# Interleaved head columns with their gate logits, rows of 640, one division per pair, and an earlier second table in an attention and expert kernel

## The chip, the cores and the metric

The kernel runs on one core of one Trainium2 chip, as one program. The metric is the device time of an execution in microseconds (us), and the time of a kernel is the median of its runs. Engines are named as the profile names them: PE (matmuls), PEld (its weight loads), DVE, ACT, POOL, and SP, which here only issues DMAs.

## The reference, cut to what matters

Attention over 8 batches, 8 heads, 576 positions and 64 columns per head comes first, and a mixture of experts with one expert per token stands on its output. In short:

```python
q_rot, k_rot = rotate(q), rotate(k)
attn = softmax(q_rot @ k_rot.T / sqrt(64))           # per batch and head
x = (attn @ v).transpose(0, 2, 1, 3).reshape(4608, 512)
logits = x @ w_gate                                   # 8 experts
e_idx = argmax(logits); gate_w = softmax(logits)[e_idx]
eom = sigmoid(x @ w_output_gate)
out[t] = gate_w[t] * eom[t, e] * (relu(x[t] @ w1[e]) @ w2[e]),  e = e_idx[t]
```

## The kernel before, in words

**Attention.** The work goes by pairs of heads, 32 of them, four to a batch. A pair has nine score tiles. For each, PE makes the scores (line 571), DVE takes the row maximum (576), ACT the exponential with its row sum (590), and DVE transposes the result by 32x32 blocks (598). PE then multiplies with the values into `acc`, one PSUM tile with a single buffer (621). At the end of a pair ACT copies `acc` to SBUF (629 to 631), and `back` writes into the same PSUM banks again: per chunk of 128 queries one PE transpose, which brings the queries to the partitions (640), and one small matmul with the gate weights, which gives that pair's share of the router's logits (642). `divide` then divides by the softmax's sums into `xb`, the batch's block in SBUF: one DVE operation for the 5x128 head columns (652) and one for the 5x32 logit shares (653). The next pair's first value matmul writes `acc` again, so it comes after `divide`. `EVENTS` is a list written out by hand that says in which of the nine steps of a pair, and at which of five places in the step, each of these parts is issued.

**Placing tokens.** When a batch is done, `place` sums the logit shares over the heads (`s0`, line 682), picks the expert (`s1` to `s8`), computes the token's gate (`s9` to `s13`), counts ranks within an expert (`s14` to `s17`) and turns token numbers into a table of lists by one-hot products (`ones` on ACT, `s20` on PE, `s21`). `store` writes `xb` to `xd` in DRAM, a row per token with its gate in the last column: 513 columns, of a block whose rows in SBUF have 640. The small arithmetic is on POOL. For the last batch these functions are not in `PLACES` but in a list, `att.last`, that the expert stage takes pieces from. Three stores of the batch before it (`late`) stand in that list too.

**Experts.** The work is in 26 slots, each of 256 or 128 tokens of one expert. A slot has eight steps j (`slot`, line 1217 on): `first` in j = 0 to 3 (`products`, line 1130 or, for 128 tokens, 1122), `second` in j = 4 to 7 (1173). At j = 4 and 5 `turn` transposes the next slot's tokens (1108). In every step ACT and DVE split a 512 KB block of weights into two parts (1092, 1094; some of the differences are on POOL), and SP loads a later one. `gather` fetches the tokens of slot s + 2 from `xd` by an indirect DMA of POOL, at j = 6; `store` scatters a finished slot's rows, also by POOL, at j = 1 and 4 of the next slot. Slots 0 to 4 hold tokens of the first six batches, by a first table of lists (`table0`) made during the attention. Slots from 5 on need the second table, `table1`: counts and slot bounds (`floor`, `sums`, `taken`, `slots`), the transposed lists written to DRAM (`turned`, 940 to 947), rows of them fetched back by indirect DMA (`rows_of`, 911 and 912) for the slots of 256 (number 2) and of 128 (number 1), and `numbers`, which subtracts and masks on POOL (921 to 924), waits some pieces, and then transposes on PE (931) and converts on DVE (932) to the row numbers that `gather` reads.

**What sets the order.** Each engine runs its instructions in program order. `table1` is a generator, cut at its `yield`s into 70 pieces; `run` takes two pieces from the list `left` at the end of every step j (three in slots 1 and 2). So slot 0 takes pieces 0 to 15, slot 1 takes 16 to 39, slot 2 takes 40 to 63, slot 3 takes 64 to 79. Before, `left` is `att.last` (46 entries with the late stores) and behind it all of `table1`: counts and the slots of number 2 are pieces 46 to 50, the transposed lists 51 and 52, `rows_of(2)` 54, the slots of number 1 at 55 to 57, `rows_of(1)` 58, `numbers(2)` 66 with its transpose at 72, `numbers(1)` 76 and 82. In a step, `turn`, `split`, `load`, `store`, `scaled` and `gather` come ahead of the pieces.

```python
left = att.last + pieces(moe.table1(), 70)
            if j == 6:
                self.gather(s + 2)
            for _ in range(per):
                if left:
                    left.pop(0)()
```

Of the kernel before, what the change touches and what calls it, by code (L numbers as in the profile page):

```python
# [23 lines left out]
P = 128  # L24
# [3 lines left out]
NCH = 5  # L28
XW = DM + 1

HL = 2 * E
RW = DM + H * HL

# [120 lines left out]
def body(ctx, tc, nb, offs, qk, v, rope, cst, gates, w, out):  # L154
# [45 lines left out]
    nc.sync.dma_start(out=stage[:, 0:nst], in_=cst[:, o:])  # L200
    nc.sync.dma_start(out=ii.rearrange("p n (h x) -> p n h x", h=2), in_=gates)

# [67 lines left out]
    if n0:  # L270
        left = att.last + pieces(moe.table1(), 70)
    else:
        left = []
        for f in att.last + pieces(moe.table1(), 70):
            f()
        moe.fetch()
        moe.gather(1)
        moe.begin0()
        moe.begin1()
# [8 lines left out]
class Attention:  # L288


    def __init__(self, tc, nb, pools, cc, ident, ii, first, trib, oneb, cnt, zero, qk, v, xd, row, lists):
# [29 lines left out]
        def newxb(b):  # L321
            xbs[b] = px2.tile([P, NCH, RW], F32, tag="xb", name=f"xb{b}")
        for n, pr in enumerate(self.pairs):
# [98 lines left out]
class Pair:  # L422
# [210 lines left out]
    def back(self):  # L633

        self.bk = self.acc.rearrange("p a b -> p (a b)")
        T, x = self.nc.tensor, [self.ac[:, c, :, :].rearrange("p a x -> p (a x)") for c in range(4)]
        x.append(self.al.rearrange("p a x -> p (a x)"))
        for cs in (range(4), (4,)):
            for c in cs:
                T.transpose(out=self.bk[0:x[c].shape[-1], c * BS:c * BS + P], in_=x[c], identity=self.ident)  # L640
            for c in cs:
                T.matmul(self.bk[0:x[c].shape[-1], c * BS + P:c * BS + P + BW], x[c], self.ii[:, self.hp, :],  # L642
                         start=True, stop=True, skip_group_check=True)

    def divide(self, xb):

        V = self.nc.vector
        heads = lambda a, x: a.rearrange("p c (h x) -> p c h x", x=x)
        r = self.rz.rearrange("p (c h) -> p c h", h=2).unsqueeze(3)
        x0, l0 = self.hp * P, DM + self.hp * 2 * HL  # L650
        five = self.bk[:, 0:NCH * BS].rearrange("p (c x) -> p c x", c=NCH)
        V.tensor_tensor(out=heads(xb[:, :, x0:x0 + P], D), in0=heads(five[:, :, 0:P], D), in1=r.broadcast_to((P, NCH, 2, D)), op=ALU.mult)
        V.tensor_tensor(out=heads(xb[:, :, l0:l0 + 2 * HL], HL), in0=heads(five[:, :, P:P + BW], HL),
                        in1=r.broadcast_to((P, NCH, 2, HL)), op=ALU.mult)

# [7 lines left out]
def place(tc, pools, pairs, b, NT, cc, trib, oneb, cnt, xbs, xd, row, lists):  # L663
# [17 lines left out]
    def s0():  # L681
        nc.vector.tensor_reduce(new("lgs", [P, NCH, 16]), xbs[b][:, :, DM:].rearrange("p c (h x) -> p c x h", x=HL), axis=AX.X, op=ALU.add)

# [53 lines left out]
    def s13(i=None):  # L737

        c = slice(0, NCH) if i is None else slice(2 * i, min(2 * i + 2, NCH))
        V.tensor_copy(xbs[b][:, c, DM], T["eg"][:, c])  # L740

# [85 lines left out]
class Moe:  # L827
# [3 lines left out]
    def __init__(self, tc, nb, pools, cc, ident, cnt, w, xd, lists, lst, out):  # L831
# [5 lines left out]
        self.rows = list_rows(nb) // P  # L837
        self.idx, self.ei, self.ri, self.tk = {}, {}, {}, {}
        self.wr, self.wp, self.xt, self.ht, self.gss, self.pys, self.hrs, self.regs, self.phs, self.ys = ({} for _ in range(10))
# [139 lines left out]
    def table1(self):  # L979
# [29 lines left out]
        yield  # L1009
        if self.n2:  # L1010
            self.rows_of(2, 2 * self.n2)
        yield
        tn, r = t([P, E], "tn"), self.padded("rn")
# [6 lines left out]
        G.tensor_tensor(out=g1, in0=g1, in1=eb, op=ALU.add)  # L1020
        yield
        d1 = self.starts("d1", g1, BIG)
        self.slots(1, e1, d1, g1[:, 0:1], 1)
        self.used = t([1, 1], "used", I32)
        G.tensor_copy(self.used, e1[0:1, E - 1:E])
        yield
        self.rows_of(1, self.n1)
        for _ in range(8):
            yield
        if self.n2:  # L1030
            yield from self.numbers(2, 2 * self.n2, 6)
# [27 lines left out]
    def gather(self, s):  # L1059
        if s >= self.end:  # L1060
            return
        n = self.NT - (2 * S if s < self.n0 else 0)
        for h in range(self.todo[s][0]):
# [33 lines left out]
    def turn(self, s, h):  # L1097
# [3 lines left out]
        if h == 0:  # L1101
            self.xt[s] = [self.buf(f"xt{i}", 0, 1, 1, [P, 4, SLOT], F32R, f"xt{i}_{s}{self.nm}") for i in range(2)]
            self.gss[s] = self.buf("gs", s, 2, 2, [P, 2], F32, f"gs{s}{self.nm}")
            V.tensor_copy(self.gss[s], self.xgs[s % 2][:, :, DM])
        xth, xtl = self.xt[s]
        tp = self.small.tile(f"mtp{s}_{h}{self.nm}")
        for dc in range(4):
            nc.tensor.transpose(out=tp[:, dc, :], in_=self.xgs[s % 2][:, h, dc * P:dc * P + P], identity=self.ident)  # L1108
        hs = slice(h * P, h * P + P)
# [107 lines left out]
    def slot(self, s, left, per=2):  # L1217
        for j in range(8):
# [15 lines left out]
            if j == 7:  # L1234
                self.scaled(s)
                if s == self.end - 1:
                    self.store(s, 0)
                    self.store(s, 1)
            if j == 6:
                self.gather(s + 2)  # L1240
            for _ in range(per):
                if left:
# [24 lines left out]
def layouts(q, k, v, wgt, wog, w1, w2):  # L1267
# [11 lines left out]
    g = np.concatenate([wgt, wog], 1).reshape(NP, 2, D, 2 * E)  # L1279
    gd = np.zeros((P, NP, 2, 2 * E), g.dtype)  # L1280
    for h in range(2):
        gd[h * D:h * D + D, :, h] = g[:, h].transpose(1, 0, 2)
    g = gd
    a = w1.reshape(E, 4, P, 4, 256).transpose(3, 0, 2, 1, 4).reshape(4, E * P, 1024)
    c = w2.reshape(E, 4, 2, P, DM).transpose(1, 0, 3, 2, 4).reshape(4, E * P, 1024)
# [23 lines left out]
```

## Time and profile before

| | |
|---|---|
| median of 3 runs | 1020.32 us (1018.58 to 1023.95) |
| the profiled execution's own time | 1015.65 us |
| its span, first to last instruction | 1013.8 us |
| mean granted TensorE clock | 0.993 |
| busy, share of the span | PE 97%, PEld 86%, DVE 76%, ACT 66%, POOL 59% |
| DMA | 216.55 MB, mean 214 GB/s |

The span is one execution on the chip. Busy time does not count the issuing of DMAs by SP or ACT, nor waits. The attention fills the span to about 514 us, the expert slots the rest. The releaser that the profile puts beside an idle time is inferred from semaphores: where an instruction waits for several, the one that came last by the profile is named, and that can be the engine's own preceding instruction.

### The profile page before, as it was taken

What the parts mean: (1) busy time and instruction counts of PE and PEld (TensorE: products, weight loads), DVE (VectorE), ACT (ScalarE), POOL (GpSimd) and SP (SyncE); (2) the same over time, 40 slices, a digit from 0 to 9 for tenths busy, and PEclk for the clock granted to TensorE, in tenths of its full rate; (3) what the DMA queues carried; (4) which work ended last, traced back from release to release, by engine and by line L of the source; (5) the groups of instructions that cost most, each with busy time, mean ns of one, the idle gap of its engine ahead of it and who ended that gap; (6) DMA issues with size and microseconds to landing.
All of it is one profiled execution on the core that took longest, in us unless ns stands there. A gap on an engine that the chain in (4) does not pass through costs nothing.

```text
span 1013.8 us, 34974 instructions
## 1 busy us (share of the span) xinstructions
PE 984.0 (97%) x14701; PEld 867.2 (86%) x14701; DVE 775.0 (76%) x1010; ACT 673.8 (66%) x1438; POOL 602.3 (59%) x708
## 2 busy tenths in 40 slices
PE   7999999999999999999999989999999999999997
PEld 6888888888888888888798878899898989899886
DVE  6889979989898988988767654657765866857673
ACT  5666686776868768686657643457666765856763
POOL 4886887878888777886615784115333543442532
PEclk9999999999999999999999998999999999999999
DMA  6554474564655455563567965657887978887780
GB/s 218 174 166 159 132 230 132 175 215 131 208 180 160 178 167 189 166 206 109 161 241 275 305 223 187 218 178 274 308 305 223 349 246 279 294 315 276 248 312 30
DMA packets 61961, 216.55 MB, mean 214 GB/s; under 512 B 7844, under 2 KB 10276, under 8 KB 61800
## 3 DMA queue, kind: packets, MB, share of 16 engines
q1 hardware_dynamic: 53360, 192.08, 57.2%
q0 software_dynamic: 7264, 21.31, 5.9%
q8 instruction: 117, 1.92, 0.8%
q10 hardware_dynamic: 1176, 0.89, 0.3%
q14 instruction: 44, 0.36, 0.1%
HBM read 196.10 MB, written 20.24 MB: 213 GB/s over the span
## 4 chain that ended last, share of the span: by engine, by line
PE 81%; ACT 7%; issue 4%; DVE 4%; POOL 2%; DMA 1%; POOLq 0%; ACTq 0%; DVEq 0%
PE sc L571 20%; PE py L1173 18%; PE acc L621 16%; PE ph L1130 14%; PE ph L1122 6%; ACT pm L590 3%; PE acc L642 3%; PE acc L640 2%; DVE m L576 2%; PE mtp L1108 1%; DVE wl L1094 1%; PE htp L1158 1%; ACT wh L1092 1%; ACT pl L795 1%; ACT ro L792 1%
## 5 line engine op out<-in xcount | busy, mean ns | idle before, releaser
L590 ACT ACTIVATE pm<-sc,m 128x576 f32<-128x576 f32 x288 | 210.8, 736 | 132.2 <-DVE m L576 129.9
L1094 DVE TENSOR_TENSOR wl<-wr,wh 128x1024 fp32r<-128x1024 f32 x183 | 229.4, 1276 | 43.6 <-ACT wh L1092 37.8
L576 DVE TENSOR_REDUCE m<-sc 128x1 f32<-128x576 f32 x288 | 207.3, 751 | 51.5 <-PE sc L571 48.0
L1173 PE MATMUL py<-wh,ht 128*128 128x512 f32 x640 | 217.3, 404 | 0.0
L1092 ACT CAST wh<-wr 128x1024 fp32r<-128x1024 f32 x208 | 211.8, 1049 | 0.0
L571 PE MATMUL sc<-kh,q 64*128 64x288 f32 x1024 | 204.2, 316 | 4.6 <-ACT pm L590 3.3
L621 PE MATMUL acc<-pt,v 32*64 32x160 f32 (+1 forms) x9216 | 198.5, 294 | 6.9 <-PE sc L571 5.6
L621 PEld LDWEIGHTS acc<-pt,v 32*64 32x64 f32 x9216 | 160.2, 131 | 30.3 <-issue 18.5
L598 DVE STREAM_TRANSPOSE pt<-pm 128x1152 f32<-128x1152 f32 x128 | 174.5, 1363 | 0.0
L571 PEld LDWEIGHTS sc<-kh,q 64*128 64x128 f32 x1024 | 147.7, 184 | 29.2 <-ACT pm L590 16.0
L1130 PE MATMUL ph<-xt,wh 128*128 128x256 f32 x896 | 161.9, 283 | 0.6 <-DVE xt L1111 0.6
L1173 PEld LDWEIGHTS py<-wh,ht 128*128 128x128 f32 x640 | 120.9, 189 | 26.6 <-DVE ht L1160 0.8
L1130 PEld LDWEIGHTS ph<-xt,wh 128*128 128x128 f32 x896 | 138.5, 189 | 3.2 <-DVE xt L1111 2.0
L1094 POOL TENSOR_TENSOR wl<-wr,wh 128x1024 fp32r<-128x1024 f32 x25 | 63.6, 2546 | 122.7 <-ACT wh L1092 115.2
L571 PE MATMUL sc<-kl,q 64*128 64x288 f32 x512 | 130.8, 292 | 0.0
L1173 PE MATMUL py<-wl,ht 128*128 128x512 f32 x320 | 126.7, 396 | 0.0
L1130 PE MATMUL ph<-xt,wl 128*128 128x256 f32 x448 | 126.1, 282 | 0.0
L1147 ACT ACTIVATE ht<-ph 128x512 fp32r<-128x512 f32 x56 | 33.4, 597 | 85.1 <-PE ph L1130 85.1
L571 PEld LDWEIGHTS sc<-kl,q 64*128 64x128 f32 x512 | 85.5, 185 | 0.0
L1130 PEld LDWEIGHTS ph<-xt,wl 128*128 128x128 f32 x448 | 84.6, 189 | 0.0
L513 POOL TENSOR_TENSOR rk<-rk,rt 128x1152 f32<-128x1152 f32 x31 | 82.1, 2649 | 0.0
L513 POOL TENSOR_TENSOR rq<-rq,rt 128x1152 f32<-128x1152 f32 x31 | 82.1, 2647 | 0.0
(255 smaller groups left out, 1517.8 us busy)
## 6 DMA issues: line engine op xcount, KB each, us to landing
wr<-in_w SPq DMA_DIRECT2D x208, 512.0 KB
v<-in_v SPq DMA_DIRECT2D x64, 576.0 KB
rk<-in_qk SPq DMA_DIRECT2D x31, 576.0 KB
rq<-in_qk SPq DMA_DIRECT2D x31, 576.0 KB
xd<-xb SPq DMA_DIRECT2D x12, 513.0 KB
xd<-xb POOLq DMA_DIRECT2D x4, 513.0 KB
xd<-xb SPq DMA_DIRECT2D x6, 128.2 KB
rk<-in_qk SPq DMA_DIRECT2D x2, 288.0 KB
```

Source lines behind the costliest of these rows:

```text
L513: self.eng(eng).tensor_tensor(out=rv, in0=rv, in1=self.rt[:, 2 * t:2 * t + 2, x], op=ALU.mult)
L571: nc.tensor.matmul(self.ps[i][:, a, :HS], st, mv, start=(n == 0), stop=(n == 2))
L576: nc.vector.tensor_reduce(self.m[i], ps[:, :, :HS], axis=AX.XY, op=ALU.max, negate=True)
L590: nc.scalar.activation(pe.rearrange("p (a b) -> p a b", a=2), self.ps[i][:, :, :HS], AF.Exp, bias=self.m[i], scale=1.0, accum_out=self.z[: ...
L598: self.nc.vector.transpose(out=self.pt[:, st[0]:st[0] + 6:5, :], in_=pe)
L621: nc.tensor.matmul(self.acc[h * D:h * D + D, a, o:o + 32 * n], self.v[r, h, j, :], self.pt[r, u:u + n, 32 * j:32 * j + 32], start=(j == 0) ...
L1092: self.nc.scalar.copy(wh, r)
L1094: eng.tensor_tensor(out=wl, in0=r, in1=wh.bitcast(F32), op=ALU.subtract)
L1122: nc.tensor.matmul(ph[:, 0, :], st[:, dc, 0:P], mv[:, dc, :], start=(n == 0), stop=(n == 11))
L1130: nc.tensor.matmul(ph[:, f, :], st[:, dc, fs], mv[:, dc, :], start=(n == 0), stop=(n == 11))
L1147: nc.scalar.activation(fl(hth[:, js, :]), fl(ph), AF.Relu)
L1173: self.nc.tensor.matmul(py[h], st[:, f, hs], mv, start=(f == 0 and n == 0), stop=(f == 7 and n == 2))
```

## The change

- **Columns.** `back`'s transposes write column x of head h to place 2x + h, so that the two heads take turns: each of the 5 transposes per pair writes PSUM with a step of two words. The gate weights are laid out the same way on the host, so the 32 logit shares stand as (x, h) right behind the 128 columns: 160 columns per chunk, contiguous in PSUM and in `xb`. The rows of w1 are put in the same order on the host.
- **Division.** `divide` is one DVE operation over 5 x 80 x 2 elements. The sums are read as pairs (h), repeated 80 times.
- **Rows.** `xb` and `xd` rows are both 640 columns: four groups of 128 head columns and 32 logit shares. The gate goes to column 128. Stores and gathers move 640 columns, and `turn` takes its four chunks of 128 at a pitch of 160. `s0` sums over two axes, of which the inner one is the pair (h).
- **Second table.** The first five pieces of `table1` run together with entries 25 to 29 of `att.last` (slot 1, j = 3 and 4). Pieces 5 to 8 stand at 46 to 49, ahead of the last batch's three stores, which move from 43 to 45 to 50 to 52. In the generator `rows_of(2)` comes after the sums of number 1 (piece 54 as before), `rows_of(1)` moves behind `numbers(2)` (to 73), `numbers(2)` begins at 64 with its transpose at 73, `numbers(1)` at 78 and 83.
- **Gathers.** `gather(s + 2)` is called at j = 0 and at j = 6, and issues once, at the first call for which the table's numbers exist. For slot 5 that is still j = 6 of slot 3; for all others it is j = 0.

```diff
-XW = DM + 1
+HW = D + 2 * E
+XW = H * HW
-RW = DM + H * HL
+WAIT = 8
...
-        left = att.last + pieces(moe.table1(), 70)
+        f, t = att.last, pieces(moe.table1(), 70)
+        for k in range(5):
+            f[25 + k] = lambda a=f[25 + k], b=t[k]: (a(), b())
+        left = f[:-4] + 4 * [f[17]] + t[5:9] + f[-3:] + t[9:]
...
-                T.transpose(out=self.bk[0:x[c].shape[-1], c * BS:c * BS + P], in_=x[c], identity=self.ident)
+                T.transpose(out=self.bk[0:x[c].shape[-1], c * BS:c * BS + P].rearrange("p (x h) -> p h x", h=2), in_=x[c], identity=self.ident)
...
-        heads = lambda a, x: a.rearrange("p c (h x) -> p c h x", x=x)
-        r = self.rz.rearrange("p (c h) -> p c h", h=2).unsqueeze(3)
-        x0, l0 = self.hp * P, DM + self.hp * 2 * HL
+        x0 = 2 * self.hp * HW
+        heads = lambda a: a.rearrange("p c (x h) -> p c x h", h=2)
+        r = self.rz.rearrange("p (c h) -> p c h", h=2).unsqueeze(2)
         five = self.bk[:, 0:NCH * BS].rearrange("p (c x) -> p c x", c=NCH)
-        V.tensor_tensor(out=heads(xb[:, :, x0:x0 + P], D), in0=heads(five[:, :, 0:P], D), in1=r.broadcast_to((P, NCH, 2, D)), op=ALU.mult)
-        V.tensor_tensor(out=heads(xb[:, :, l0:l0 + 2 * HL], HL), in0=heads(five[:, :, P:P + BW], HL),
-                        in1=r.broadcast_to((P, NCH, 2, HL)), op=ALU.mult)
+        self.nc.vector.tensor_tensor(out=heads(xb[:, :, x0:x0 + 2 * HW]), in0=heads(five[:, :, 0:2 * HW]),
+                                     in1=r.broadcast_to((P, NCH, HW, 2)), op=ALU.mult)
...
-        nc.vector.tensor_reduce(new("lgs", [P, NCH, 16]), xbs[b][:, :, DM:].rearrange("p c (h x) -> p c x h", x=HL), axis=AX.X, op=ALU.add)
+        nc.vector.tensor_reduce(new("lgs", [P, NCH, 16]), xbs[b].rearrange("p c (q x) -> p c q x", q=NP)[:, :, :, P:].rearrange("p c q (x h) -> p c x q h", h=2), axis=AX.XY, op=ALU.add)
...
-        if self.n2:
-            self.rows_of(2, 2 * self.n2)
-        yield
         tn, r = t([P, E], "tn"), self.padded("rn")
...
+        if self.n2:
+            self.rows_of(2, 2 * self.n2)
+        yield
         d1 = self.starts("d1", g1, BIG)
...
-        self.rows_of(1, self.n1)
-        for _ in range(8):
+        for _ in range(WAIT):
             yield
         if self.n2:
-            yield from self.numbers(2, 2 * self.n2, 6)
-        for _ in range(4):
+            yield from self.numbers(2, 2 * self.n2, 9)
+        self.rows_of(1, self.n1)
+        for _ in range(5):
             yield
-        yield from self.numbers(1, self.n1, 6)
+        yield from self.numbers(1, self.n1, 5)
...
-        if s >= self.end:
+        if s >= self.end or s in self.got or self.todo[s][1] not in self.idx:
             return
+        self.got.add(s)
...
-            if j == 6:
+            if j in (0, 6):
                 self.gather(s + 2)
```

## Rows read from the trace of the kernel before

**Rows 1.** Busy time in stretches: start:end, length, PE, PEld, DVE, ACT, POOL, clock, DMA, GB/s

```profile
46.00:107.00 61.00, 60.14 (x1497) 52.23 (x1497) 55.20 (x73) 40.17 (x110) 44.28 (x35) 1.00 0.49 158
565.16:588.95 23.79, 23.79 (x157) 21.57 (x156) 16.05 (x18) 12.36 (x18) 19.74 (x50) 1.00 0.95 308
588.95:620.74 31.79, 26.23 (x156) 23.01 (x155) 14.68 (x17) 11.95 (x16) 22.68 (x50) 0.89 0.56 178
620.74:644.50 23.76, 23.76 (x155) 21.38 (x155) 14.69 (x17) 11.79 (x16) 5.03 (x4) 1.00 0.66 222
```

**Rows 2.** Timeline of PE in slot 3, with idle time and releaser in brackets

```profile
603.49 0.66 PE L1108 MATMUL mtp<-ident,xg 128*128 128x128 f32 x4 [0.23 <-DMA xg<-xd,0idx]
609.48 0.29 PE L931 MATMUL 2tr<-ident,2tk 18*128 18x18 f32 x1 [5.34 <-POOL 2tk L921]
```

**Rows 3.** Busy time in stretches, columns as in rows 1, cut by POOL's work

```profile
553.77:569.22 15.45, 15.45 (x89) 13.19 (x88) 8.51 (x10) 12.43 (x25) 10.11 (x15) 1.00 0.92 252
569.22:583.73 14.51, 14.51 (x101) 13.33 (x100) 9.76 (x12) 7.40 (x12) 12.29 (x42) 1.00 1.01 327
583.73:601.37 17.64, 17.64 (x125) 16.43 (x124) 10.86 (x12) 9.34 (x13) 13.94 (x37) 1.00 0.67 207
601.37:605.64 4.27, 2.54 (x13) 1.65 (x11) 1.75 (x2) 2.20 (x3) 3.32 (x6) 1.00 0.84 271
605.64:609.42 3.78, 0.00 (x0) 0.00 (x0) 1.89 (x3) 0.07 (x1) 3.52 (x5) 0.70 0.54 183
```

**Rows 4.** What wrote tile xg: count, duration ns min/median/max, first and last start

```profile
L1064 POOL DMA_INDIRECT xg<-xd,0idx x10: 1008/1120/1813, 499.8 to 600.1; - x10
```

**Rows 5.** Timeline of POOL in slot 0

```profile
525.07 2.67 POOL L1094 TENSOR_TENSOR wl<-wr,wh 128x1024 fp32r<-128x1024 f32 x1 [4.36 <-ACT wh L1092]
530.30 1.17 POOL L688 TENSOR_TENSOR dd<-lgs,mx 128x40 f32<-128x40 f32 x1 [2.57 <-DVE mx L685]
...
538.94 1.81 POOL L1064 DMA_INDIRECT xg<-xd,0idx  x1 [0.52 <-issue]
541.05 1.45 POOL L1064 DMA_INDIRECT xg<-xd,0idx  x1 [0.30 <-issue]
```

**Rows 6.** The chain that ended last, in slot 0: start, length, what

```profile
530.30 1.18 POOL dd L688
...
531.51 0.24 ACT ex L691
...
536.60 0.50 ACT pl L795
...
537.15 0.39 PE pl L802
```

**Rows 7.** Timeline of DVE at the end of a pair

```profile
182.29 0.78 DVE L652 TENSOR_TENSOR xb<-acc,rz 128x640 f32<-128x640 f32 x1
183.00 0.31 DVE L653 TENSOR_TENSOR xb<-acc,rz 128x160 f32<-128x160 f32 x1
```

**Rows 8.** What wrote and read tile xb, columns as in rows 4

```profile
L653 DVE TENSOR_TENSOR xb<-acc,rz x32: 305/307/316, 45.5 to 519.3; 128x160 f32<-128x160 f32 x32
...
L682 DVE TENSOR_REDUCE lgs<-xb x8: 1214/1223/1253, 97.9 to 528.7; 128x80 f32<-128x640 f32 x8
```

**Rows 9.** Timeline of PE behind the division of rows 7

```profile
183.59 0.67 PE L621 MATMUL acc<-pt,v 32*64 32x160 f32 x27 [0.32 <-PE sc L571]
```

**Rows 10.** Waits of PE from 30 to 514 us: total us, times, longest

```profile
PE acc L621 <- PE sc L571: 5.6, 17, 0.4
```

**Rows 11.** Instructions of line 640, columns as in rows 4

```profile
L640 PE MATMUL acc<-ident,ac x128: 272/273/330, 42.4 to 517.0; 128*128 128x128 f32 x128
L640 PE MATMUL acc<-ident,al x32: 277/277/277, 43.7 to 518.0; 128*64 128x128 f32 x32
```

**Rows 12.** The chain that ended last, through one pair's back

```profile
180.60 0.81 PE acc L642 x8
181.41 0.11 PE acc L640
```

More of the change, by code (lines that the diff above doesn't have):

```diff
@@ L200, in body @@
     nc.sync.dma_start(out=stage[:, 0:nst], in_=cst[:, o:])
-    nc.sync.dma_start(out=ii.rearrange("p n (h x) -> p n h x", h=2), in_=gates)
+    nc.sync.dma_start(out=ii.rearrange("p n (x h) -> p n x h", h=2), in_=gates)
     consts = [
@@ L321, in newxb @@
         def newxb(b):
-            xbs[b] = px2.tile([P, NCH, RW], F32, tag="xb", name=f"xb{b}")
+            xbs[b] = px2.tile([P, NCH, XW], F32, tag="xb", name=f"xb{b}")
         for n, pr in enumerate(self.pairs):
@@ L645, in divide @@
     def divide(self, xb):
-        V = self.nc.vector
-        heads = lambda a, x: a.rearrange("p c (h x) -> p c h x", x=x)
-        r = self.rz.rearrange("p (c h) -> p c h", h=2).unsqueeze(3)
-        x0, l0 = self.hp * P, DM + self.hp * 2 * HL
+        x0 = 2 * self.hp * HW
+        heads = lambda a: a.rearrange("p c (x h) -> p c x h", h=2)
+        r = self.rz.rearrange("p (c h) -> p c h", h=2).unsqueeze(2)
         five = self.bk[:, 0:NCH * BS].rearrange("p (c x) -> p c x", c=NCH)
-        V.tensor_tensor(out=heads(xb[:, :, x0:x0 + P], D), in0=heads(five[:, :, 0:P], D), in1=r.broadcast_to((P, NCH, 2, D)), op=ALU.mult)
-        V.tensor_tensor(out=heads(xb[:, :, l0:l0 + 2 * HL], HL), in0=heads(five[:, :, P:P + BW], HL),
-                        in1=r.broadcast_to((P, NCH, 2, HL)), op=ALU.mult)
+        self.nc.vector.tensor_tensor(out=heads(xb[:, :, x0:x0 + 2 * HW]), in0=heads(five[:, :, 0:2 * HW]),
+                                     in1=r.broadcast_to((P, NCH, HW, 2)), op=ALU.mult)
 def number(NT, b):
@@ L739, in s13 @@
         c = slice(0, NCH) if i is None else slice(2 * i, min(2 * i + 2, NCH))
-        V.tensor_copy(xbs[b][:, c, DM], T["eg"][:, c])
+        V.tensor_copy(xbs[b][:, c, P], T["eg"][:, c])
     def store(i):
@@ L837, in __init__ @@
         self.rows = list_rows(nb) // P
-        self.idx, self.ei, self.ri, self.tk = {}, {}, {}, {}
+        self.idx, self.ei, self.ri, self.tk, self.got = {}, {}, {}, {}, set()
         self.wr, self.wp, self.xt, self.ht, self.gss, self.pys, self.hrs, self.regs, self.phs, self.ys = ({} for _ in range(10))
@@ L1103, in turn @@
             self.gss[s] = self.buf("gs", s, 2, 2, [P, 2], F32, f"gs{s}{self.nm}")
-            V.tensor_copy(self.gss[s], self.xgs[s % 2][:, :, DM])
+            V.tensor_copy(self.gss[s], self.xgs[s % 2][:, :, P])
         xth, xtl = self.xt[s]
@@ L1107, in turn @@
         for dc in range(4):
-            nc.tensor.transpose(out=tp[:, dc, :], in_=self.xgs[s % 2][:, h, dc * P:dc * P + P], identity=self.ident)
+            nc.tensor.transpose(out=tp[:, dc, :], in_=self.xgs[s % 2][:, h, 2 * HW * dc:2 * HW * dc + P], identity=self.ident)
         hs = slice(h * P, h * P + P)
@@ L1238, in slot @@
                     self.store(s, 1)
-            if j == 6:
+            if j in (0, 6):
                 self.gather(s + 2)
+            assert j < 7 or s + 2 >= self.end or s + 2 in self.got
             for _ in range(per):
@@ L1279, in layouts @@
     g = np.concatenate([wgt, wog], 1).reshape(NP, 2, D, 2 * E)
-    gd = np.zeros((P, NP, 2, 2 * E), g.dtype)
+    gd = np.zeros((P, NP, 2 * E, 2), g.dtype)
     for h in range(2):
-        gd[h * D:h * D + D, :, h] = g[:, h].transpose(1, 0, 2)
+        gd[h * D:h * D + D, :, :, h] = g[:, h].transpose(1, 0, 2)
     g = gd
+    w1 = w1.reshape(E, 4, 2, D, FF).transpose(0, 1, 3, 2, 4)
     a = w1.reshape(E, 4, P, 4, 256).transpose(3, 0, 2, 1, 4).reshape(4, E * P, 1024)
```

## The prediction

> **What bounds the kernel.** I read the time by stages first. In a typical stretch of the attention PE is busy 60.14 of 61 us, and in the slots it is busy all the time except in one [rows 1]. So PE sets the pace almost everywhere: work taken from DVE, ACT or POOL pays only where PE waits for it, and work added to PE pays in full. The exception is slot 3, from 588.95 to 620.74 us: 31.79 us against 23.79 for the slot before it and 23.76 for the one behind, with PE busy 26.23 us and a mean granted clock of 0.89 where its neighbours have 1.00 [rows 1]. The timeline of PE says what it waited for: 5.34 us for POOL's `2tk`, that is `numbers(2)`, the second table's last arithmetic, and just before 0.23 us for slot 4's gather [rows 2]. The rest of the 8.0 us is PE's restart at the lower of its two clock levels. The reader should see that this is one stall, at one place, with its clock cost.
>
> Why POOL is late: from 569.22 us, where `table1` begins, to 609.42 us, where `numbers(2)` ends, POOL's stretches follow one another with little room: 12.29 us busy in 14.51, 13.94 in 17.64, 3.32 in 4.27, 3.52 in 3.78 [rows 3], and the difference is the issue gaps between small instructions. Ahead of that, from 553.77 to 569.22, it is busy for only 10.11 of 15.45 us [rows 3].
>
> **Part 1, the second table.** The change puts the 14.51 us from 569.22 to 583.73 (counts, `taken`, `sums`, `slots(2)`) at slot 1, j = 3, directly behind `s17`, which ends at 553.77. It takes the stretch from 601.37 to 605.64 (`rows_of(1)` and an output store) out from in front of `numbers(2)`. It also takes slot 3's gather out of the stretch from 553.77 (that gather goes to j = 0 of slot 1). What stood in that stretch is then 10.11 - 2 x 1.12 [rows 4] = 7.9 us, and with nine DMA issues at a gap of 0.30 each [rows 5] 10.6 us. POOL's new sum is 553.8 + 10.6 + 14.5 + 17.6 (the stretch from 583.73: `rows_of(2)`, `taken`, `sums`, `slots(1)`, slot 4's gather) + 3.8 (`numbers(2)`) = 600.3 us. PE asks for the result behind the first half of `turn(4)`, at 603.95 us (0.23 earlier without the wait for the gather). The spare is about 3.5 us, so the stall goes. The waits inside the new order are met: the lists' transposes move from piece 51 to 46, eight pieces ahead of `rows_of(2)`, and the last batch's three stores, now behind them, are read first by slot 5's gather, which stays at j = 6 of slot 3. Nothing on PE, ACT or DVE waits for the stores. `numbers(1)` follows with its own transpose at piece 83, in slot 4, where POOL is busy 5.03 of 23.76 us [rows 1]. Slot 3 goes from 31.79 to about 23.8 plus 0.2 for the transpose that stays: **-7.8 us**. Bounds: -8.0, and 0 if POOL is late by as much as before.
>
> **Part 2, gathers at j = 0.** In slots from 4 on POOL has room (5.03 of 23.76), and a gather that passes one output store (which waits for its slot's end anyhow) costs nothing; the cover is that idle time. In slots 1 and 2 it is in the sum of part 1. In slot 0 it is not free: slot 2's gather now stands ahead of `s2`, the last batch's `dd`. POOL finishes a weight difference at 525.07 + 2.67 = 527.74 and then idles 2.57 us until DVE's maximum lets `dd` go at 530.30 [rows 5]. The two gathers take 0.52 + 1.81 + 0.30 + 1.45 = 4.1 us as they stood, or 0.52 + 1.12 + 0.30 + 1.12 = 3.1 at the median [rows 4, 5], so `dd` starts at 530.8 to 531.8 in place of 530.3. Behind `dd`, ACT waits with `ex`, and behind `ex` in its queue stand the `pl` products that PE takes at 537.15, 0.05 us after ACT's last one ends [rows 6]: PE has no slack there. So the price is 0.5 to 1.5 us; I take **+0.8**, nearer the median gather. As the 1.17 us of `dd` may hold a delay that the gather takes over, the low end is 0.3.
>
> **Part 3, one division.** Two operations from start to end take 183.31 - 182.29 = 1.02 us [rows 7]. By 0.78 us for 640 and 0.31 for 160 elements [rows 7, 8] an element costs 0.99 ns and an operation 0.15 us, so 800 in one are 0.94 us: 0.08 less. PE does feel it. The next pair's first `acc` matmul starts at 183.59 after 0.32 us idle [rows 9], right behind the division's end, and `acc` has one buffer. The profile names PE's own score matmul as the releaser, but that one had ended when the idle time began. There are 17 such waits, 5.6 us in all [rows 10]. So 17 x 0.08 = **-1.3 us**; with all 32 pairs it would be -2.6. The other end: `s0` takes 1.22 us for 640 elements that it reads singly, 16 words apart [rows 8]; at that rate 800 are 1.53 us, 0.51 more than now, x 32 = +16 us. I take the first, as the new operation reads `acc` and writes `xb` without gaps, as rows 7 do, and only the sums come in pairs.
>
> Here a rule bears on the choice. The Trainium skill, Vector Engine (DVE) Microarchitecture Reference, section 5.2 (Measured stream behaviour on trn2), says that a port keeps its full rate when words come in adjacent pairs from an 8-byte boundary, and loses it on single hops. By that rule both the sums' pairs and the new `s0` run at full rate, and the sum is the one above with the -1.3; the row of `s0` agrees as to single hops.
>
> `s0` itself may fall from 1.22 towards 0.8 us or stay; either way it is off the path (eight times in all, and the last one ends before the gathers of part 2 do): 0.
>
> **Part 4, stepped transposes.** 160 PE transposes [rows 11] now write every second word. No row shows a stepped PE write. One costs 0.11 us on the chain, and the small matmuls of 32 columns, a quarter of the columns, cost 0.81 / 8 = 0.10 [rows 12]: the pace of both is thus hardly set by the columns written, but by what each instruction loads, and slower writing has that to hide under. From below I take 0 (nothing in it is shorter), from above a doubling, 160 x 0.11 = 17.6 us. I take **0**, by that near row.
>
> **Part 5, rows of 640.** Stores and gathers carry 640 / 513 = 1.25 times the bytes. Stores have whole steps until a reader comes, and gathers now 6 steps more; the DMA share around is 0.49 to 0.95 [rows 1]. 0; should the cover go, a gather that lands late shows as the 0.23 us of rows 2.
>
> **Sum.** -7.8 + 0.8 - 1.3 = -8.3 us. Against the profiled execution's own time, 1015.65 us (span 1013.8 us, 1.85 around it), that gives 1007.4. The median shown, 1020.32, stands 4.7 above that execution; I carry the difference over: **1012.0 us**. A measurement here can tell about 0.5%, some 5.1 us.
>
> **Rivals.**
> A. *POOL is still late.* The spare is 3.5 us on a queue of some 46 us, and POOL's gathers alone vary from 1.0 to 1.8 us [rows 4]. If POOL's new stretch takes 15% more (7 us), PE waits some 3.5 us and restarts slowly: about half of the 7.8 stays, -4.5 + 0.8 = about 1016.5. For it: every long POOL item of the stretch is moved, not removed. Against it: nine pieces now lie between the arithmetic and its transpose, in place of six.
> B. *Stepped writes cost (slower).* Each transpose takes twice as long, on PE, which has no slack: +17.6 - 8.3 = +9.3, 1029.6 us. It decides from 8.3 / 160 = 0.05 us more per transpose on. For it: PE is the bound, and no row shows such a write. Against it: rows 12, the pace that does not follow the columns.
> The Trainium skill, SBUF — State Buffer, section Door 1 (The DMA port swizzle), has a note that PSUM is accessed in lines of two fp32 words and that any PSUM pattern with gaps slows matmuls significantly, without a figure. By that rule rival B would be the forecast; no run here shows it yet.
> C. *The one division is slow.* At the rate of `s0`, +16 + 1.3 - 8.3 = +9.0, 1029.3 us. Against it: only two of ten sums are read per step, and the large streams have no gaps.
>
> **How the numbers follow.** Forecast 0.69, A 0.15, B 0.10, C 0.06. Faster by over 0.5%: the forecast, less the 0.03 in which parts 2 and 4 eat over 3 us of it, plus the third of A with the shortest wait (0.04): 0.70. Slower: most of B and C, 0.13; the partial sizes of all three make 0.17 for no change. The range: best case -8.0 - 2.6 + 0.3 = -10.3, or 1010.0, and a median that scatters like the runs shown (1.7 below) gives 1008; upwards it takes in A and small prices of B and C, to 1020. Left out are most of B and C and a little below.
>
> **What would show it.** Right: slot 3 as long as its neighbours, no PE wait at `2tr`, POOL's `2tk` ending near 600 us; `dd` at about 531 and a PE wait of up to 1.5 us before `pl`; 32 divisions of about 0.94 us and the waits of rows 10 near 4.3 us; transposes still 0.11 us apart. Wrong: a PE idle time before `2tr` (A), transposes at 0.2 us apart (B), a division over 1.1 us (C), or a new wait in the slots with 128 tokens.

## The result, and the profile after

The kernel after takes 1008.42 us (median of 7 runs, 1007.29 to 1022.82), the kernel before, run beside it, 1018.58 us (7 runs, 1015.91 to 1023.95). The ratio is 0.9906, 95% interval 0.9886 to 0.9925: faster, by 7.6 to 11.6 us. The profiled execution took 1007.78 us, its span is 1006.0 us (1013.8 before) and its mean clock 0.996 (0.993). The longest of the seven runs after ran in the chip's slower state, at a mean clock of 0.975, and is left out of the ratio.

That lies inside the range forecast, 3.6 us under the value forecast; 1.7 of these are the kernel before itself, which takes 1018.58 us over seven runs where the forecast started from 1020.32. But the trace shows that the terms did not do it as forecast. First the stretches that answer to [rows 1]: the attention, and slots 1, 2... counted as there, each cut at a slot's first `ph` matmul. Columns: start:end, length, PE, PEld, DVE, ACT, POOL, clock, DMA share, GB/s.

```profile
46.00:107.00 61.00, 60.30 (x1505) 52.14 (x1509) 55.28 (x70) 40.66 (x111) 45.07 (x37) 1.00 0.49 158
562.06:585.71 23.65, 23.65 (x157) 21.59 (x156) 16.11 (x19) 12.57 (x18) 16.03 (x37) 1.00 0.89 314
585.71:610.11 24.40, 23.73 (x154) 21.37 (x153) 15.08 (x17) 11.79 (x16) 18.28 (x38) 1.00 0.74 260
610.11:639.94 29.83, 26.12 (x155) 23.73 (x154) 14.78 (x17) 11.81 (x16) 12.95 (x13) 0.89 0.61 202
```

The third row is slot 3: 24.40 us where [rows 1] have 31.79. The stall is gone from there but for 0.68 us. The fourth row is slot 4: 29.83 us where [rows 1] have 23.76, with a clock of 0.89. That is the same picture as slot 3 before, one slot later. PE's timeline says what it waits for in the two slots (idle time and releaser in brackets):

```profile
601.13 0.23 PE L935 MATMUL 2tr<-ident,2tk 18*128 18x18 f32 x1 [0.68 <-POOL 2tk L925]
...
619.68 0.28 PE L935 MATMUL 1tr<-ident,1tk 15*128 15x15 f32 x1 [3.71 <-POOL 1tk L925]
619.89 0.58 PE L1135 MATMUL ph<-xt,wh 128*128 128x256 f32 x1
```

The first row answers to the 5.34 us of [rows 2]. The second is new: the transpose of `numbers(1)`. The third shows the lower of the two clock levels (1.2 GHz) behind it: one `ph` matmul takes 0.58 us, and 0.28 us at full clock. The granted clock is 0.50 from 619.89 to 624.90 us and 1.00 from 625.20 on. POOL's timeline tells why `1tk` is late:

```profile
550.70 0.20 POOL L787 TENSOR_TENSOR lo<-lo,po 128x5 f32<-128x5 f32 x1
...
584.80 1.63 POOL L1192 DMA_INDIRECT out<-y,0idx  x1 [4.32 <-DVE wl L1099]
...
600.63 0.45 POOL L925 TENSOR_TENSOR 2tk<-2tk,2g 18x128 f32<-18x128 f32 x1
601.50 1.14 POOL L1192 DMA_INDIRECT out<-y,0idx  x1 [0.43 <-ACT xt L1115]
605.48 0.99 POOL L1192 DMA_INDIRECT out<-y,0idx  x1 [2.84 <-DMA out<-y,0idx]
...
606.97 1.49 POOL L916 DMA_INDIRECT 1tl<-lst,1ri  x1 [0.31 <-issue]
...
608.97 1.73 POOL L916 DMA_INDIRECT 1tk<-lst,1ri  x1 [0.31 <-POOL 1tk L915]
...
615.29 0.97 POOL L926 TENSOR_TENSOR 1tk<-1tk,1tl 15x128 f32<-15x128 f32 x1 [1.91 <-DMA 1tk<-lst,1ri]
...
619.18 0.44 POOL L925 TENSOR_TENSOR 1tk<-1tk,1g 15x128 f32<-15x128 f32 x1
```

The first row is the end of `s17`. `numbers(2)` ends at 601.08. Then come two output stores, the second after 2.84 us of idle time for which the trace names the first one's DMA. Only then comes `rows_of(1)`, from 606.47 to 610.70, then the gather of slot 5, then the wait for `1tk`'s own landing, then 4.3 us of arithmetic, which ends at 619.62. PE had asked at 615.97.

The whole account of the two profiled executions, in us, cut at the first and last division of the attention and at ACT's first `y` operation of each slot:

| stretch | before | after | difference |
|---|---|---|---|
| start to first division | 44.75 | 45.42 | +0.67 |
| first to last division | 473.77 | 469.59 | -4.18 |
| last division to first `y` (slot 0) | 23.40 | 24.04 | +0.64 |
| slots 1 and 2 | 46.53 | 46.16 | -0.37 |
| slot 3 | 31.63 | 24.41 | -7.22 |
| slot 4 | 23.77 | 29.81 | +6.05 |
| slots 5 to 25 | | | -3.40 |
| behind them | 6.45 | 6.45 | 0.00 |

The differences add up to -7.81, that of the spans. Of the -4.18 not all belongs to the change: the execution before had a mean clock of 0.91 from 125 to 145 us, where the one after has 1.00. The +0.67 ahead of it is no effect of the change that a trace could show: over the ten profiles of this document the first division starts between 44.50 and 46.14 us. The experiments take the rest apart.

What became of the other steps. The one division and the shorter `s0` (count, duration in ns min/median/max, first and last start), against 0.78 + 0.31 and 1223 ns in [rows 7, 8]:

```profile
L657 DVE TENSOR_TENSOR xb<-acc,rz x32: 950/952/993, 45.4 to 515.0; 128x800 f32<-128x800 f32 x32
L686 DVE TENSOR_REDUCE lgs<-xb x8: 776/777/805, 98.0 to 525.2; 128x80 f32<-128x640 f32 x8
```

PE's transposes of 128 columns, which now write every second word, against the first row of [rows 11]:

```profile
L646 PE MATMUL acc<-ident,ac x128: 271/273/332, 43.1 to 513.5; 128*128 128x128 f32 x128
```

And one pair's `back` on PE's timeline, first in the kernel before, then in the kernel after:

```profile
179.94 0.66 PE L640 MATMUL acc<-ident,ac 128*128 128x128 f32 x4
180.43 0.98 PE L642 MATMUL acc<-ii,ac 128*128 128x32 f32 x8
181.25 0.28 PE L640 MATMUL acc<-ident,al 128*64 128x128 f32 x1
```

```profile
178.40 0.66 PE L646 MATMUL acc<-ident,ac 128*128 128x128 f32 x4
178.89 0.98 PE L648 MATMUL acc<-ii,ac 128*128 128x32 f32 x8
179.71 0.28 PE L646 MATMUL acc<-ident,al 128*64 128x128 f32 x1
```

The starts stand 0.49 and 0.82 us apart in both: the step of two words costs nothing that a trace can show.

In slot 0, POOL, then DVE, then PE, against [rows 5, 6]:

```profile
521.56 2.67 POOL L1099 TENSOR_TENSOR wl<-wr,wh 128x1024 fp32r<-128x1024 f32 x1 [4.82 <-ACT wh L1097]
524.39 1.86 POOL L1069 DMA_INDIRECT xg<-xd,0idx  x1 [0.15 <-issue]
526.55 1.75 POOL L1069 DMA_INDIRECT xg<-xd,0idx  x1 [0.30 <-issue]
528.33 0.27 POOL L692 TENSOR_TENSOR dd<-lgs,mx 128x40 f32<-128x40 f32 x1
```

```profile
525.25 0.81 DVE L686 TENSOR_REDUCE lgs<-xb 128x80 f32<-128x640 f32 x1
526.09 0.20 DVE L689 TENSOR_REDUCE mx<-lgs 128x5 f32<-128x40 f32 x1
```

```profile
534.27 0.40 PE L806 MATMUL pl<-ro,pl 64*128 64x290 f32 x1 [0.81 <-ACT pl L799]
```

From the end of `wl` to the end of `dd` 4.37 us pass (3.73 before, by [rows 5]), and PE has a wait of 0.81 us at `pl` that it did not have. `dd` follows the second gather, which ends at 528.30; the maximum that it waited for in [rows 5] is ready at 526.29, 2 us earlier.

### The profile page after: what moved, and what is told of

It reads as the page before. It is cut to its first block, busy times and chain, and to the rows that moved or that the text cites. A ratio compares the mean times of both kernels' runs of the same rounds, so it can differ in the third digit from the quotient of the medians.

```text
span 1006.0 us, 34949 instructions
## 1 busy us (share of the span) xinstructions
PE 978.1 (97%) x14701; PEld 865.7 (86%) x14701; DVE 771.2 (77%) x978; ACT 674.7 (67%) x1438; POOL 607.8 (60%) x708
## 5 line engine op out<-in xcount | busy, mean ns | idle before, releaser
L1178 PE MATMUL py<-wh,ht 128*128 128x512 f32 x640 | 214.6, 400 | 0.0
L627 PE MATMUL acc<-pt,v 32*64 32x160 f32 (+1 forms) x9216 | 196.4, 293 | 5.7 <-PE sc L577 3.8
L1153 DVE SCALAR_TENSOR_TENSOR ht<-ph,ht 128x512 fp32r<-128x512 f32 x56 | 38.7, 691 | 56.9 <-ACT ht L1152 56.2
```

Of the source, the lines that this page charges most:

```text
L627: nc.tensor.matmul(self.acc[h * D:h * D + D, a, o:o + 32 * n], self.v[r, h, j, :], self.pt[r, u:u + n, 32 * j:32 * j + 32], start=(j == 0) ...
L1153: nc.vector.scalar_tensor_tensor(out=fl(htl[:, js, :]), in0=fl(ph), scalar=0.0, in1=fl(hth.bitcast(F32)[:, js, :]), op0=ALU.max, op1=ALU.s ...
L1178: self.nc.tensor.matmul(py[h], st[:, f, hs], mv, start=(f == 0 and n == 0), stop=(f == 7 and n == 2))
```

## The experiments

The first four take the change apart, the next four test what these left open. All times are against the kernel before, run beside them on the same chip: 1016.83 us (26 runs) beside the first four, 1020.27 us (11 runs) beside the other four.

### The later transpose of numbers(1)

The kernel after, with one number changed:

```diff
-        yield from self.numbers(1, self.n1, 5)
+        yield from self.numbers(1, self.n1, 12)
```

> The changed kernel, with the transpose of numbers(1) seven pieces later (piece 90, slot 4 j = 5, in place of 83, slot 4 j = 1). Theory: the 6.05 us that slot 4 became longer are PE's wait of 3.71 us for 1tk and its restart at the lower clock, so slot 4 goes from 29.8 to about 23.7 us and the span falls by 6 us against the changed kernel (ratio to the kernel before near 0.985). Rival 1: the next thing is late in its place (slot 5's tokens, fetched only behind rows_of(1) at 611 to 613 us), then PE waits at turn(5) and only 2 to 3 us are won. Rival 2: the clock falls by itself at this place, then nothing is won.

Measured: 1003.7 us (1000.4 to 1008.08, 6 runs), ratio 0.9869, interval 0.9831 to 0.9907, span 1001.8 us. Slots 3 and 4, columns as above:

```profile
587.46:611.86 24.40, 23.74 (x155) 21.37 (x154) 15.07 (x17) 11.78 (x16) 17.91 (x38) 1.00 0.76 261
611.86:635.58 23.72, 23.72 (x155) 21.34 (x153) 14.68 (x17) 11.81 (x16) 13.01 (x13) 1.00 0.75 249
```

Slot 4 is 23.72 us in place of 29.83, PE busy all the time, at full clock. So the 3.71 us wait and the half clock behind it, 6.1 us together, come from the piece at which PE asks for `1tk`, and from nothing else in the slot. The ratios alone would not settle it: 0.9869 here and 0.9906 for the changed kernel are 3.8 us apart, and their intervals overlap.

### The columns alone

The changed kernel with the order of the second table and the gathers put back:

```diff
-        left = f[:-4] + 4 * [f[17]] + t[5:9] + f[-3:] + t[9:]
+        left = att.last + pieces(moe.table1(), 70)
...
-            if j in (0, 6):
+            if j == 6:
```

> The kernel before with the columns, the rows of 640, the single division and the summing over pairs alone: table and gathers as before. Theory: each of the 32 pairs becomes 0.08 us shorter, so the attention falls by 2.6 us and nothing else changes: -2.6 us, slot 3 still with its wait of 5.3 us. Rival 1 (the prediction's): only the 17 pairs with a listed wait gain, -1.3 us. Rival 2: the slots from 5 on, 3.4 us shorter in the changed kernel, owe this to the rows of 640 or to the place of the buffers; then this kernel shows up to -6 us.

Measured: 1011.28 us (9 runs), ratio 0.995, interval 0.9925 to 0.9974, span 1008.9 us. From first to last division it takes 469.88 us (473.77 before), from there to the first `y` 22.97 us (23.40 before, 24.04 after). Slot 3 is 32.32 us: with the old order the stall stays, and PE, which comes a little earlier, waits a little longer. Slots 5 to 25 are 1.25 us shorter than before. So of slot 0 two things are told apart: the columns give 0.43 us there, and what else the change does takes 1.07 us on top of them.

### The gathers alone

The kernel before, with the gathers called at j = 0 and 6:

```diff
...
-            if j == 6:
+            if j in (0, 6):
                 self.gather(s + 2)
```

> The kernel before with the gathers at j = 0 alone. Theory: slot 0 becomes 0.6 us longer (dd behind the gather), and the slots of 256 tokens behind two slots of 128 (9, 14, 19, 24) go from 22.2 to 21.6 us, since POOL's weight differences at j = 7 no longer stand behind a gather: together -1.5 us. Rival: those slots stay at 22.2 us, and their gain in the changed kernel comes from the rows of 640; then this kernel is 0.6 us slower than before.

Measured: 1011.43 us (12 runs), ratio 0.995, interval 0.9928 to 0.9971, span 1009.0 us. Slots 5 to 25 are 2.05 us shorter: 0.46 to 0.51 in each of slots 9, 14 and 24, and 0.49 in 18 and 19 together; 9, 14, 19 and 24 are the slots of 256 tokens behind two of 128. Slot 3 is 29.84 us: its wait for the gather is gone and POOL is a little sooner. PE's short waits behind 660 us (three for `xt`, 0.6 us in all) are gone. They stood at the starts of slots 9, 14 and 24. In the kernel before, at slot 9:

```profile
716.27 0.28 PE L1130 MATMUL ph<-xt,wh 128*128 128x256 f32 x1
716.74 0.38 PE L1130 MATMUL ph<-xt,wh 128*128 128x256 f32 x1 [0.19 <-DVE xt L1111]
716.96 0.28 PE L1130 MATMUL ph<-xt,wl 128*128 128x256 f32 x1
```

From start to start that is 0.47 and 0.22 us, where `ph` matmuls usually stand 0.12 apart: the wait that is listed with 0.19 us costs 0.45. The three waits are thus nearly the whole gain in these three slots. What changes in slots 18 and 19, where no wait is listed, is not shown.

In slot 0 nothing is lost, where 0.6 us were expected: the first `y` comes 23.41 us after the last division (23.40 before). POOL's timeline there:

```profile
524.19 2.67 POOL L1095 TENSOR_TENSOR wl<-wr,wh 128x1024 fp32r<-128x1024 f32 x1 [5.88 <-ACT wh L1093]
527.02 1.85 POOL L1065 DMA_INDIRECT xg<-xd,0idx  x1 [0.16 <-issue]
529.18 1.00 POOL L1065 DMA_INDIRECT xg<-xd,0idx  x1 [0.31 <-issue]
530.20 0.41 POOL L688 TENSOR_TENSOR dd<-lgs,mx 128x40 f32<-128x40 f32 x1
```

From the end of `wl` to the end of `dd` 3.75 us, as before (3.73): the second gather took 1.00 us here, and `dd` itself 0.41 in place of 1.17. In the four runs that have the columns and this gather ahead of `dd`, the second gather takes 1.75 us. So the gathers' price in slot 0 is 0.01 us without the columns and 1.07 with them; why the second gather takes longer there was not tried.

### The second table's order alone

The kernel before with the new order of `left` and of the generator, and the gathers at j = 6:

```diff
-        left = att.last + pieces(moe.table1(), 70)
+        left = f[:-4] + 4 * [f[17]] + t[5:9] + f[-3:] + t[9:]
...
-            yield from self.numbers(2, 2 * self.n2, 6)
+            yield from self.numbers(2, 2 * self.n2, 9)
+        self.rows_of(1, self.n1)
...
```

> The kernel before with the second table's new order alone. Theory: the wait only moves: slot 3 falls from 31.7 to about 24.4 us, slot 4 rises from 23.8 to about 29.8, net -1.2 us. Rival: it is the gathers at j = 0 that push rows_of(1) and numbers(1) back on POOL; then slot 4 stays under 25 us here and the kernel is 6 to 7 us faster than before.

Measured: 1018.04 us (12 runs), ratio 1.0001, interval 0.9976 to 1.0025, span 1017.0 us: no change. Slots 2, 3 and 4, and PE's wait in slot 2:

```profile
565.86:592.49 26.63, 24.06 (x157) 21.56 (x157) 15.95 (x19) 12.43 (x18) 19.51 (x44) 1.00 0.94 279
592.49:617.61 25.12, 23.84 (x154) 21.37 (x153) 14.59 (x17) 11.78 (x16) 18.61 (x33) 1.00 0.74 244
617.61:647.57 29.96, 26.25 (x155) 23.80 (x154) 14.79 (x17) 11.79 (x16) 11.32 (x12) 0.89 0.58 186
```

```profile
583.16 0.66 PE L1111 MATMUL mtp<-ident,xg 128*128 128x128 f32 x4 [2.57 <-DMA xg<-xd,0idx]
```

Slot 3 loses most of its stall (PE still waits 1.28 us at `2tr`), slot 2 gains a wait of 2.57 us, and slot 4 becomes 6 us longer. The wait in slot 2 is for slot 3's gather, which now stands behind five pieces of `table1` on POOL and is issued at 574.69 (558.88 in the kernel before). So the earlier table needs the gathers at j = 0, which keep slot 2 free of this wait; the gathers do not need the table, as the run above shows.

### One division or two

The changed kernel with its division cut again:

```diff
-        self.nc.vector.tensor_tensor(out=heads(xb[:, :, x0:x0 + 2 * HW]), in0=heads(five[:, :, 0:2 * HW]),
-                                     in1=r.broadcast_to((P, NCH, HW, 2)), op=ALU.mult)
+        for a, n in ((0, D), (P, 2 * E)):
+            self.nc.vector.tensor_tensor(out=heads(xb[:, :, x0 + a:x0 + a + 2 * n]), in0=heads(five[:, :, a:a + 2 * n]),
+                                         in1=r.broadcast_to((P, NCH, n, 2)), op=ALU.mult)
```

> The changed kernel with its one division cut in two operations again, in the new layout: columns 0 to 128 of each chunk, then 128 to 160. Theory: one division is worth its 0.08 us on every pair, since the next pair's first acc matmul comes right behind it everywhere, not only at the 17 waits that the profile listed: 32 x 0.08 = +2.6 us in the attention against the changed kernel, about 0.08 us in nearly every pair. Rival, the prediction's own term: only 17 pairs feel it, +1.3 us. Rival, that the shorter attention comes from something else in the columns (a cheaper s0, the reads of rows): 0.

Measured: 1010.5 us (4 runs), ratio 0.9899, interval 0.9852 to 0.9947, span 1008.4 us. A single execution cannot tell 1.3 from 2.6 us: the five profiled kernels with one division take 469.59, 471.54, 469.88, 473.70 and 474.95 us from the first division to the last, although they have the same instructions there. The longer ones show stretches with a granted clock below 1 (0.97 from 230 to 291 us and 0.83 from 506 to 520 us in the longest). So I compare pair by pair where none of the three executions is disturbed. The divisions of pairs 18 and 22, one batch apart, before, after and in this run:

```profile
319.99 0.79 DVE L652 TENSOR_TENSOR xb<-acc,rz 128x640 f32<-128x640 f32 x1
...
381.14 0.78 DVE L652 TENSOR_TENSOR xb<-acc,rz 128x640 f32<-128x640 f32 x1
```

```profile
318.24 0.95 DVE L657 TENSOR_TENSOR xb<-acc,rz 128x800 f32<-128x800 f32 x1
...
379.12 0.95 DVE L657 TENSOR_TENSOR xb<-acc,rz 128x800 f32<-128x800 f32 x1
```

```profile
319.90 1.01 DVE L658 TENSOR_TENSOR xb<-acc,rz 128x640 f32<-128x640 f32 x2
...
381.05 1.02 DVE L658 TENSOR_TENSOR xb<-acc,rz 128x640 f32<-128x640 f32 x2
```

A batch of four pairs takes 61.15, 60.88 and 61.15 us: two divisions in the new layout give back exactly what one had gained, 0.27 us a batch. It is not the same in each pair: the four intervals are 15.97, 15.30, 14.91 and 14.97 us before and 15.97, 15.24, 14.79 and 14.88 after, so one of the four gains nothing. Over all: the shortest interval between each two neighbouring divisions, over the five profiles with two divisions, adds up to 469.67 us; over the five with one, to 467.26 us. That is 2.41 us in 31 intervals; sums of the medians in place of the shortest differ by 2.45. So one division is worth **-2.4 us** by the traces, and nothing else in the columns shows in the batch compared. The ratios do not show it (0.9899 here, 0.9906 for the changed kernel), and slot 4 happens to be 1.3 us shorter here, 28.53 us, with a wait of 3.31 us for `1tk` in place of 3.71. PE's waits for `acc` from 30 to 514 us go with it (total, times, longest), in the changed kernel and then in this run; [rows 10] have 5.6, 17:

```profile
PE acc L627 <- PE sc L577: 3.8, 13, 0.3
```

```profile
PE acc L627 <- PE sc L577: 6.5, 22, 0.4
```

### The buffer of gathered rows

In every run with rows of 640 the `py` matmuls follow one another at 0.230 us, and at 0.232 in those with rows of 513 (means of the distances under 0.3 us; the medians are 0.231 and 0.232). The kernel before with a wider buffer and the same 513 columns in it:

```diff
-        xg = self.px2.tile([P, 4, XW], F32, tag="xg", name="xg", bufs=1)
-        self.xgs = [xg[:, 0:2, :], xg[:, 2:4, :]]
+        xg = self.px2.tile([P, 4, 640], F32, tag="xg", name="xg", bufs=1)
+        self.xgs = [xg[:, 0:2, 0:XW], xg[:, 2:4, 0:XW]]
```

> The kernel before with the buffer of gathered rows 640 columns wide, of which the same 513 are filled: nothing moves but the places of the buffers behind it in SBUF. Theory: the pitch of the py matmuls, which fell from 0.232 to 0.230 us (median) in every run with rows of 640, follows these places: 0.230 here too, 0.14 to 0.19 us off every slot of 256 tokens. Rival, that it follows the longer rows themselves or the pitch of 160 in the transposes' input: 0.232 and no change of any slot.

Measured (one execution): 1016.2 us, span 1014.4 us. The pitch is 0.230 us, and slots 5 to 25 are 1.06 us shorter than before, with -0.14 to -0.21 in slots 6, 9, 11, 14, 16 and 21. Slots 1 and 2 are 0.35 us shorter, as in the changed kernel (0.37). So this gain does not come from longer rows being stored and gathered, but from the wider buffer: its own row pitch, or the places of the buffers behind it. Which of the two was not tried.

### rows_of(1) first

The changed kernel with `rows_of(1)` ahead of `numbers(2)` again:

```diff
+        self.rows_of(1, self.n1)
         for _ in range(WAIT):
...
-        self.rows_of(1, self.n1)
         for _ in range(5):
```

> The changed kernel with rows_of(1) put back ahead of numbers(2), as it stood before; the pieces at which the transposes ask stay. Theory: the new wait of slot 4 (3.71 us, and half the clock behind it) is there because rows_of(1) now queues on POOL behind numbers(2) and two output stores. With it first, 1tk is done before piece 83 asks, and slot 4 is 23.7 us (29.8 in the changed kernel); but its two gathers, 4.2 us of POOL, then stand ahead of 2tk, which ends near 605 in place of 601.1: PE waits some 4.5 us at 2tr, and slot 3 is 29 to 31 us in place of 24.4. So the sum is about that of the changed kernel. Rival, that slot 4's wait comes from numbers(1)'s transpose being asked for too early whatever stands before it: slot 4 keeps over half of its 6 us.

Measured (one execution): 1011.45 us, span 1009.7 us. Slots 3 and 4, and PE's wait in slot 3:

```profile
590.20:619.95 29.75, 25.31 (x155) 22.52 (x154) 15.03 (x17) 11.78 (x16) 23.11 (x43) 0.94 0.66 226
619.95:643.58 23.63, 23.63 (x155) 21.33 (x153) 14.84 (x18) 11.79 (x16) 6.67 (x8) 1.00 0.75 237
```

```profile
609.38 0.23 PE L935 MATMUL 2tr<-ident,2tk 18*128 18x18 f32 x1 [4.44 <-POOL 2tk L925]
```

Slot 4 is whole again and slot 3 is not. So it is `rows_of(1)`, moved behind `numbers(2)` and the two stores, that made slot 4's wait; the same POOL work makes one stall or the other, as long as the pieces at which PE asks stay where they are.

### The pieces that ask, moved

The changed kernel with both transposes later, and slot 2's gather behind `dd`:

```diff
-            yield from self.numbers(2, 2 * self.n2, 9)
+            yield from self.numbers(2, 2 * self.n2, 11)
...
-        yield from self.numbers(1, self.n1, 5)
+        yield from self.numbers(1, self.n1, 10)
...
-            if j in (0, 6):
+            if j in ((0, 6) if s else (2, 6)):
```

> The changed kernel with three pieces of order moved: the transpose of numbers(2) two pieces later (piece 75, the last one ahead of slot 5's gather), the transpose of numbers(1) at piece 90 in slot 4 (in place of 83), and in slot 0 alone the gather at j = 2 in place of j = 0, so that it stands behind the last batch's dd. Theory: each remaining wait in this region is a question of which piece asks before POOL is done. Slot 4 is 23.7 us as in the run with the later numbers(1) (29.8 in the changed kernel); slot 3 loses its 0.68 us wait at 2tr and the stretch at half clock behind it, 24.4 to about 23.5; slot 0 loses the 0.81 us wait at pl, of which 0.64 us came with the change. Together about -6.1 - 0.9 - 0.6 = -7.6 us against the changed kernel, some 1001 us. Rival, that slot 0's 0.64 us come from the columns and not from the gather ahead of dd: slot 0 stays and the sum is -7.0. Rival, that the later transpose of numbers(2) makes slot 5's gather late: a new wait at mtp in slot 4, 1 to 2 us.

Measured: 1001.93 us (999.69 to 1003.84, 6 runs), ratio 0.9815, interval 0.9779 to 0.985, span 1001.5 us: the lowest median of this study. Slots 3 and 4, and POOL in slot 0:

```profile
587.99:611.61 23.62, 23.62 (x154) 21.37 (x153) 15.07 (x17) 11.77 (x16) 17.60 (x36) 1.00 0.76 248
611.61:635.33 23.72, 23.72 (x154) 21.35 (x153) 14.67 (x17) 11.80 (x16) 14.78 (x15) 1.00 0.79 264
```

```profile
524.85 2.68 POOL L1099 TENSOR_TENSOR wl<-wr,wh 128x1024 fp32r<-128x1024 f32 x1 [4.89 <-ACT wh L1097]
529.66 1.17 POOL L692 TENSOR_TENSOR dd<-lgs,mx 128x40 f32<-128x40 f32 x1 [2.12 <-DVE mx L689]
```

PE has no listed wait left from 525 to 665 us. From the end of `wl` to the end of `dd` it is 3.30 us, and from the last division to the first `y` 22.97, as with the columns alone. So the 1.07 us of slot 0 are the two gathers ahead of `dd`, and slot 5's gather is not late. Against the changed kernel the stretches give -1.07 in slot 0, -0.78 in slot 3 and -6.10 in slot 4, -7.95 together, where -7.6 was expected.

## Why the prediction was right, and where it was not

The direction, the size and the range held. That the sum did so was luck: a loss of 6 us that it lacked met gains of about 5 us that it also lacked (3.40 in slots 5 to 25, 0.37 in slots 1 and 2, 1.1 in the division).

**Part 1 failed at one sentence**: that `numbers(1)` "follows with its own transpose at piece 83, in slot 4, where POOL is busy 5.03 of 23.76 us". That row is the load of slot 4 in the kernel before, where `rows_of(1)` had been fetched one slot earlier. The change moves this stretch behind `numbers(2)`, as the prediction itself had said when it took it out of the way of `numbers(2)`. It did not ask who waits for it there. The working that was missing: `2tk` done at about 601, two stores with a wait between (about 5 us), `rows_of(1)` (4.2 us), a gather, the landing and 4.3 us of arithmetic end near 620; piece 83 stands at the end of slot 4's j = 1, six of 23.7 us into the slot, near 616. Cost: +6.05 us, shown twice, by the later transpose and by `rows_of(1)` put first.

The first half of part 1 was right, but without any spare: slot 3 went from 31.63 to 24.41, -7.2 for -7.8. `2tk` ended at 601.08 where 600.3 was forecast, but that close agreement is luck too, since the execution stood 2.9 us earlier by then: `s17` ended at 550.90 and not at 553.77. From there POOL took 50.2 us, where the sum has 46.5. PE asked after 49.6 us; by [rows 2] it should have been 50.1, as 609.48 less 5.34 is 604.14, not 603.95, and the wait for the gather is gone. The 3.7 us more on POOL ate the spare of 3.5. The forecast sum counted busy time and issue gaps, and had no term for an output store that waits on the queue: 4.32 us idle before the store at 584.80. So rival A came true in small: PE waits 0.68 us, and slot 3 is 0.78 us shorter where the transpose is asked for later. (Rival A's own sum leaves out the -1.3: half of 7.8 with the other two terms is -4.4, or 1015.9 us.)

**Part 2** was right in slot 0 as to the mechanism and its size: the stretch is 0.64 us longer than before, for +0.8 (0.5 to 1.5, low end 0.3). `dd` starts 0.03 us behind the second gather; the two gathers took 1.86 and 1.75 us, the slower of the two pairs of durations weighed. That the `dd` of 1.17 us holds a delay that a gather can take over was right as well: it took 0.27 behind the gathers, and 1.17 again where the gather was put behind it. In the later slots the price was not 0 but a gain of 2 us (the gathers alone: -2.05 in slots 5 to 25). "Costs nothing" was argued, and what moving a gather gives was not asked.

**Part 3** had the right operation and the wrong count. The duration came out at 0.952 us for 0.94 forecast. But the count of waits that a profile lists is no count of the pairs that wait: shorter ones are not listed, and they shrink too. The term was -1.3 and measured -2.4, near the -2.6 that the prediction gave for all 32 pairs, though not by 0.08 in each: in the batch shown one interval gains nothing and one 0.12.

**`s0`** was put off the path, and in the changed kernel it is, for the reason given: it falls from 1223 to 777 ns, but the last one and its maximum end at 526.29, and `dd` waits for the gathers until 528.30. In the run with the columns alone, where no gather stands ahead of `dd`, the same `s0` is on the path, and slot 0 gains 0.43 us. As to the speed, the rule quoted from the Trainium skill (Vector Engine (DVE) Microarchitecture Reference, section 5.2) holds here: 640 elements in adjacent pairs take 777 ns, and the old division took 785 ns for as many in a row. Rival C falls with it.

**Part 4** was right: 0. Transposes of 273 ns before and after, and the same distances. The note of the Trainium skill (SBUF — State Buffer, section Door 1) that any PSUM pattern with gaps slows matmuls significantly does not show in these writes of every second word; the measurement decides, and rival B falls.

**Part 5** had no late gather, as forecast, but the wider buffer gave 1.06 us in slots 5 to 25, and 0.35 in slots 1 and 2, that nothing in it foresaw. Of the 3.40 us in slots 5 to 25, 0.29 are left that neither this nor the gathers explain.

Summed by stretches, without the first division's start and with -2.4 for the attention: -2.4 + 0.64 - 1.54 - 3.40 = -6.7 us. The medians say -7.6 to -11.6. What the remaining 1 to 5 us are is open. The clock in the attention, which differs from one execution to the next, is not all of it: of the executions with a clock of 1.00 from 46 to 514 us, the three with two divisions take 473.02, 473.14 and 474.12 us from the first division to the last, and the two with one 469.59 and 469.88, which is 3.1 to 4.5 us and not 2.4.

## What to carry to other kernels

When a step is moved behind another on a queue, write down who waits for the moved step, at which place in its own order it asks, and compare that time with the new sum of the queue; the load of the old kernel in that stretch says nothing about it. A late result can be cured on the asking side: here two numbers that put two transposes a few pieces later took 6.9 us off slots 3 and 4, where the reordering had won 1.2 net. Whether they would have done so in the kernel before, without the reordering, was not tried. To price a small operation that recurs, compare undisturbed intervals between its occurrences over several profiles, not the waits that the profile lists: it leaves out short ones, and shows others too short (0.19 us listed, 0.45 from start to start).

## What was not expected of the hardware

- PE's transposes of 128 columns write every second word of PSUM at the pace of adjacent ones (128 of them, 273 ns median both ways, four in 0.66 us).
- Two output stores of POOL with 2.84 us of idle time between them, for which the trace names the first one's DMA: a queue with such stores cannot be summed from busy times.
- A PE wait of 3.71 us cost 6.1, as matmuls ran at the lower clock level behind it (slot 4, mean clock 0.89); one of 2.57 us in slot 2 of the run with the table's order alone cost 2.8, with a mean clock of 1.00.
- The pace of the `py` matmuls changes by 1% (0.232 to 0.230 us) when a buffer in SBUF that they do not read becomes wider.
